# Weight unpacking with the shift inside the joining instruction, one score step for both heads, and a new order table

## The chip, the cores and the metric

The kernel runs on one core of a Trainium2 chip. The metric is the time of the program on the device, in microseconds (us). The engines are TensorE (PE, matmuls; its weight loads are PEld), VectorE (DVE), ScalarE (ACT), GpSimd (POOL) and SyncE (SP), which issues the DMAs here.

## The reference

Attention with two kinds of masks, then two dense layers with squared ReLU, then two with SiLU, all in float32 (B, H, S, D = 4, 8, 576, 64; the layers are 512 to 2048 to 512 over 2304 tokens):

```
scores = q @ k.T / sqrt(64)
rel = pos[:, None] - pos[None, :]
mask = (rel >= 0) & (rel < 32)                       # heads 0 to 3
mask = (rel >= 0) & (rel < 128) & (rel % 4 == 0)     # heads 4 to 7
attn = softmax(where(mask, scores, -1e9)) @ v        # heads side by side: x, 2304 x 512
h = x @ w_in;  x = (relu(h) * relu(h)) @ w_out       # first layer pair
h = x @ w_in2; out = (h * sigmoid(h)) @ w_out2       # second layer pair
```

The weights arrive as 64-bit words (float64), two 32-bit words each.

## The kernel before, in words

Every float32 matmul operand of the layers is split into a high and a low half that PE takes at full rate, and a product is three matmuls (high by high, high by low, low by high; lines 788 to 790, 836 to 838). The layers run over token tiles. The first three tiles of 256 tokens of the first layer pair (`mlp`) run together with the attention of the early tokens and with the loading of the weights; this is the first stage, to about 215 us. Then come three tiles of 512 with one level of Strassen's scheme (`mlp2`, to 480 us), and three tiles of 768 for the second layer pair (`strassen`, to the end).

The attention goes by half sequences (h from 0 to 7, 288 queries each) and pairs of heads. For a pair, the score matmuls (line 533) have 64 rows of contraction, one head in partitions 0 to 63 and the other in 64 to 127; a plain pair has three units, a dilated pair four. As float32 each of these matmuls is two in the trace. DVE masks the scores and takes their extremes (line 558, tiles `ap`, `ast`), for the first eight pairs a subtraction follows (lines 691 on DVE, 694 on POOL), then PE transposes, ACT takes the exponential, PE multiplies by the values (738, 625) and the result is normalised.

Weights are unpacked by `weights`, 64 pieces of 128 x 512: the DMA brings `raw`; the high word is scaled into `cv` (line 282 on ACT, 284 elsewhere, called top); the low word is scaled in place (290 on ACT, 292 elsewhere, called low); `cv` is shifted by 3 (302, or POOL's form on `raw`, 304); the sign is put in (311 or 314); and the low word is added (318, on DVE or POOL, called the join). A cast to the high half (245, 247, 249) and a subtraction for the low half (252) follow.

Nothing is scheduled on the chip by chance: `ORDER` is a table that lists all operations with the engine they run on (P for PE, A for ACT, V for DVE, G for POOL, D for a DMA issued by SP) and the place of their buffers; `F14` is 14 filler matmuls on PE (line 1245). Each engine runs its own entries in the order of the table, and waits for the data. A POOL entry also waits for the last DVE entry ahead of it that is marked as locking their port. `APART` names the half sequences whose score step is two operations, one for each head.

Of the kernel before, what the change touches and what calls it, by code (L numbers as in the profile page):

```python
# [12 lines left out]
I32 = mybir.dt.int32  # L13
# [164 lines left out]
class Kern:  # L178
# [76 lines left out]
    def weights(self, m, c, key, dkey, js=(0, 1)):  # L255
# [3 lines left out]
        for j in js:  # L259
# [10 lines left out]
            vi = lambda cv=cv: cv.tile.bitcast(I32)  # L270
# [37 lines left out]
            def sign(e, vi=vi, pair=pair, b=b):  # L308
# [9 lines left out]
            w = self.op({"DVE": c_dve(n), "Pool": c_pool2(n)}, lambda e, vi=vi, pair=pair: self.eng[e].tensor_tensor(  # L318
                out=vi(), in0=vi(), in1=pair(I32)[:, :, 0], op=ALU.add), [s, z], k, [], [cv, raw], "w" + at, True)
# [1040 lines left out]
P10@3 P36@28@1 V17 V50 P67@36@2 G20 A12 V38 A11 V49 V37 D65@156 V48 P13@0 V39 V68 V40 D95@152 P21@1 F3@3 V51 A22  # L1360
P41@2 A23 D96@160 V35 V14 P24@3 V71 A43 V15 G127@0 V70 A42 A16@2 V81 D398@196 V79 P52@1 V69 V82 P44@2 V80 A53
V25 A54 V72 A136@4 P55@0 V26 V45 V66 V46 A27 V83 D143@52 P98@40@3 V56 V138 A47@6 V57 P28@1 G129 P73@3 V100
A29@44 F3@2 V58 A74 V101 D160@76 P59@2 V111 A31@48 V99 P84@3 V32 A62 V30 A60 P75@0 A85 V102 V61 A128 F3@1 V63
V110 D152@56 P86@2 V76 V103 A137 V77 V112 P104@1 A78@8 V113 V87 F7@3 V97 V114 V88 A105 V130 D177@88 A89 P115@1
V139 P106@0 A116 V131 F1@2 P90@3 D169@80 P117@2 V140 A91@60 A93@64 A132@68 F5@1 V94 V92 A141@164 V107 V118
P400@3@1@72@0 V108 V119 D211@124 G133 A153@14 V109@12 V120 A162 V403 F2@2 V401 A145 P121@0 G142 V402 V410
D506@201 P404@2 V411 A122 A144@10 V123 V412 A154 V146 P1238@3 D186@92 V399 A161@2 V147 A170@0 V148 P413@1 A124
A405 V178@4 D220@128 A149@84 V125 V163 A1239@16 P406@0 V150 A414 A1240 V164 P415@2 A179 D194@108 V407 V155
P1244@3 A1241@6 V408 V165 A409@8 V416 V156 A166@100 D424@196 P507@0@1@96@1 V417 V1242 A418 V157 P1243 A1245@18
V167 A158@168 D151 V172 A1246 V510 A187@10 D134 P419@3 V159 P1250@2 A422@104 A420 V512 A1247@12 G189 V508 V423  # L1370
A513 V421 A171 D203@116 V1248 P426@3@0@112@2 V180 A1251@16 V173 A511 P1249 A509 V427 G174 V523 A1252 V428 A188
V429 V436 V438 A1253@14 P430@2 V525 A524 V437 V514 V521 A526 V515 V425 V1254 A522 P439@1 V190 A431 A516 V527
A517 V175@172 P432@3 V528 V176 A440 A529 P518@0 V530 A222 P441@2 V433 V181 A204@2 P531@1 P1255 V434 V442 A520
V182 A435@8 V443 V519 A533 V444 D539@196 A532 A183@120 V191 P534@3 A195@6 V184 P445@0 A537@12 A535 V446 P1256@1
A192@176 G197 V448 V536 A196 V447 D450@201 V449 V198 A205 V193 A1257@18 P540@0@3@20@3 A1258 V199 A1259@4 D237@40
A212@0 V1260 V554 A200@28 P1261 V556 G206 V545 A557 V558 V543 A555 D254@76 V541 V201 A559 P452@0@3@24@0 A542
V560 V207 A544 A546 V561 D538 V451 P1262@1 V208 D271@112 A562 A563 V547 V465 V548 V455 A549 V466 G550 V454
# [12 lines left out]
P640@3 A627 A1282 V628 V641 P1273 A608 V645 A1283@14 V615 V652 V629 G1284 V616 V654 A630 V643 V656 P1303 V289@2  # L1390
V617 A1305@18 A297@4 V291 V292 P618@0 A1295@6 P1285 A642 V1306 A646 V293 A619 A298 V283 P631@0 P1310@2 A657
V277@132 A653 V284 A632 D339@124 V1296 A285@40 P633@0 V278 A655 V299 P1297 A644 A634 D185 V647 V286 A294@136
A1307@14 V635 D666@201 P1316@1 A1311@16 V306@6 A1312 V648 V658 A636@10 V659 V1308 A660 V295 P1322@2 D287
V1550@12 A649 D637 V308 A1317@18 V1551@2 P661@0 A1313@0 P650@3 P1309 A662 V307 A315 V1314 V1552@112 A651 V324
A1318 P667@3@76@1 V1554@108 A1323@16 V1553 A1324 V300 A1319@8 P663@1 A314@10 V669 P668@0 V1555 V673 A664@2 V1320
P1328@2 V682 V671 V680 D694@196 A672 V684 V316 A674 P1334@3@0@1 V301 A670 A1329@18 V309 A302@72 D665 V675 A1330
P1315 V676 D253 A685 V677 A1559 V303 D330@92 A1331@12 A1556 P678@2 V1332 P1321 V323@0 A1325@14 V317 A681 A679
V1326 A683 P1340@2 V1562@8 A1335@16 A1336 V310 V686 P695@3@20@2 V1563@2 A1341@18 A1342 V687 V1560 A688 P696@2
V701 V703 G1564@116 V697 A702 P1333 V712 A311@144 V714 V1557 A1337@4 D1561 A704 V699 V710 P1327 A715 V325 A700
V1338 V716 V318 D1558 P689@3 A1343@14 V312 P1346@2 A698 A711 V705 V341 A690 V706 V1565 A717 P1352@3 V707  # L1400
A1347@16 A1348 V1566@36 A713 V1344 A319@68 V1567 P708@2 P1339 V326 A709 A1353@18 V320 A1568 D347@112 V718
# [12 lines left out]
P786@2 A1419@18 V371 A1420 P1393 V1603 A1397@8 A787@0 V1398 A1604 V1593 A374@6 D820@196 P1412@3 V1596 A1607
# [259 lines left out]
```

## Time and profile before

| | us |
|---|---|
| three runs | 848.31, 849.13, 851.52 (median 849.13) |
| the profiled execution | 849.5 |
| its span in the trace | 847.7 |
| PE, DVE, ACT, POOL busy in the span | 839.2, 638.8, 501.5, 122.2 |

Busy time of an engine is the union of its instructions; PE's matmuls overlap each other, so the step from one start to the next tells what one costs. A wait is put down to the engine that released it last.

### The profile page before, as it was taken

The numbers are of one execution on the slowest core, as the hardware profiler recorded it, in microseconds if no ns is written. First come the engines' busy times: TensorE is split into PE (matmuls) and PEld (weight loads), VectorE is DVE, ScalarE is ACT, GpSimd is POOL, SyncE is SP. The second block draws the span as 40 slices with busy tenths as digits, with TensorE's granted clock in tenths as the row PEclk, the third lists the DMA queues.
The fourth block names the chain that finished last, engine by engine and source line by source line (L and its number), as shares of the span: only waits on it lengthen the run. The fifth ranks groups of instructions, "written<-read, shape, count | busy, mean of one in ns | idle before, by whom it ended". The sixth has DMA issues, their size and how long they took to land.

```text
span 847.7 us, 16967 instructions
## 1 busy us (share of the span) xinstructions
PE 839.2 (99%) x6009; PEld 795.6 (94%) x6009; DVE 638.8 (75%) x1706; ACT 501.5 (59%) x1324; POOL 122.2 (14%) x142
## 2 busy tenths in 40 slices
PE   9989999999999999999999999999999999999998
PEld 7879999999989889889998999999999999999998
DVE  6999999888888698768899997578722488422765
ACT  5999988887666265334542566565445555345652
POOL 2220000101210202131201002102201111202020
PEclk9999999999999999999999999999999999999999
DMA  9585568879898888988999989889774774773441
GB/s 344 178 284 207 152 204 304 278 265 333 310 303 318 308 292 282 326 311 288 336 344 299 343 308 351 301 287 324 248 259 149 246 266 164 269 262 111 174 159 65
DMA packets 83603, 223.56 MB, mean 264 GB/s; under 512 B 8768, under 2 KB 18240, under 8 KB 83520
## 3 DMA queue, kind: packets, MB, share of 16 engines
q1 hardware_dynamic: 83520, 222.49, 75.2%
q8 instruction: 47, 0.77, 0.3%
q14 instruction: 36, 0.29, 0.1%
HBM read 172.13 MB, written 50.33 MB: 262 GB/s over the span
## 4 chain that ended last, share of the span: by engine, by line
PE 94%; ACT 3%; DVE 1%; issue 0%; POOL 0%; POOLq 0%; ACTq 0%
PE y L1094 17%; PE sa L1179 15%; PE s L936 15%; PE y L1179 6%; PE y L990 5%; PE y L991 5%; PE y L992 5%; PE sa L1094 4%; PE s L788 3%; PE s L789 2%; PE s L790 2%; PE ax L533 2%; PE y L836 2%; PE ax L625 2%; PE y L837 2%; PE y L838 2%
## 5 line engine op out<-in xcount | busy, mean ns | idle before, releaser
L245 ACT CAST hl<-gq 128x384 fp32r<-128x384 f32 x168 | 79.5, 513 | 58.7 <-PE sa L1179 28.6
L1094 PE MATMUL y<-xs,ws 128*128 128x384 f32 x552 | 107.5, 334 | 0.0
L252 DVE TENSOR_TENSOR hl<-gq,hl 128x384 fp32r<-128x384 f32 x144 | 78.9, 581 | 27.3 <-ACT hl L245 24.0
L1094 PEld LDWEIGHTS y<-xs,ws 128*128 128x128 f32 x552 | 96.6, 188 | 0.1
L1065 DVE TENSOR_TENSOR gq<-y,gq 128x384 f32<-128x384 f32 x46 | 25.0, 554 | 94.1 <-PE y L1094 82.9
L1070 ACT COPY gq<-y 128x384 f32<-128x384 f32 x92 | 42.7, 479 | 75.0 <-PE y L1094 67.6
L1179 PE MATMUL sa<-hl,wp 128*128 128x384 f32 x432 | 79.1, 334 | 0.0
L936 PE MATMUL s<-x,ws 128*128 128x256 f32 x576 | 76.2, 284 | 0.0
L990 PE MATMUL y<-g,w 128*128 128x512 f32 x192 | 76.2, 397 | 0.0
L1179 PEld LDWEIGHTS sa<-hl,wp 128*128 128x128 f32 x432 | 75.2, 188 | 0.0
L991 PE MATMUL y<-g,w 128*128 128x512 f32 x192 | 75.2, 392 | 0.0
L992 PE MATMUL y<-g,w 128*128 128x512 f32 x192 | 74.9, 390 | 0.0
L952 DVE TENSOR_TENSOR h<-s,h 128x512 f32<-128x512 f32 x96 | 59.4, 619 | 19.8 <-PE s L936 16.6
L936 PEld LDWEIGHTS s<-x,ws 128*128 128x128 f32 x576 | 72.2, 191 | 1.2
L245 ACT CAST g<-r 128x256 fp32r<-128x256 f32 (+1 forms) x86 | 42.9, 504 | 51.2 <-DVE r L972 42.8
L566 ACT ACTIVATE ap<-ap,ast 96x128 f32<-96x128 f32 (+3 forms) x168 | 62.2, 371 | 8.3 <-DVE ast L575 4.2
L788 PE MATMUL s<-x,w 128*128 128x256 f32 x192 | 56.4, 294 | 0.1
L790 PE MATMUL s<-x,w 128*128 128x256 f32 x192 | 54.3, 283 | 0.0
L789 PE MATMUL s<-x,w 128*128 128x256 f32 x192 | 54.2, 282 | 0.0
L1179 PE MATMUL y<-hl,sw 128*128 128x384 f32 x288 | 51.4, 334 | 0.0
L1179 PE MATMUL sa<-hl,sw 128*128 128x384 f32 x288 | 50.9, 334 | 0.0
L1179 PEld LDWEIGHTS y<-hl,sw 128*128 128x128 f32 x288 | 50.0, 188 | 0.0
(176 smaller groups left out, 2071.2 us busy)
## 6 DMA issues: line engine op xcount, KB each, us to landing
raw<-w SPq DMA_DIRECT2D x64, 512.0 KB, 6.3
ws<-w1x SPq DMA_DIRECT2D x48, 512.0 KB, 6.7
ws<-w2x SPq DMA_DIRECT2D x48, 512.0 KB, 5.4
sw<-w2y SPq DMA_DIRECT2D x48, 512.0 KB, 4.5
wa<-w1s SPq DMA_DIRECT2D x24, 512.0 KB, 6.8
wa<-w2s SPq DMA_DIRECT2D x24, 512.0 KB, 5.7
w1x<-st SPq DMA_DIRECT2D x16, 512.0 KB, 4.8
w2x<-st SPq DMA_DIRECT2D x16, 512.0 KB, 5.1
```

The costliest lines, as they stand in the source:

```text
L245: self.nc.scalar.copy(out=out, in_=in_)
L252: self.eng[eng].tensor_tensor(out=out, in0=a, in1=b, op=ALU.subtract)
L566: es.append(self.op({"ACT": c_act(nk) + 0.185}, lambda e, i=i, n=n, c=c, p=p, st=st: nc.scalar.activation(out=p.tile[:n, c], in_=p.tile[:n ...
L788: nc.tensor.matmul(o, wh.tile[:, s], xh, start=(kk == 0), stop=False)
L789: nc.tensor.matmul(o, wh.tile[:, s], xl, start=False, stop=False)
L790: nc.tensor.matmul(o, wl.tile[:, s], xh, start=False, stop=(kk == KC - 1))
L936: nc.tensor.matmul(bank.tile[:, o:o + 256], wp, xp, start=i == 0, stop=last, skip_group_check=True)
L990: nc.tensor.matmul(o, wh.tile[:, s], gh.tile, start=c == 0, stop=False)
L991: nc.tensor.matmul(o, wh.tile[:, s], gl.tile, start=False, stop=False)
L992: nc.tensor.matmul(o, wl.tile[:, s], gh.tile, start=False, stop=(c == NF - 1))
L1094: nc.tensor.matmul(o, w[part == 2].tile[:, kk * P:kk * P + P], x[b][part == 1].tile[:, kk * half:kk * half + half], start=new and not kk a ...
L1179: nc.tensor.matmul(o, u.tile[:, c * P:c * P + P], v.tile, start=new and not q and not part, stop=q == nf - 1 and part == 2, skip_group_che ...
```

## The change

The operation `low` is gone, 64 of them. The join is a single DVE instruction that shifts the low word right by 29 and combines it with `cv` by a bitwise or; it can no longer run on POOL. `APART` is empty, so the fourth half sequence (h = 3) issues its scores for both heads in one operation, the heads in turn. The order table is another one; it has 3899 entries where 3969 stood, 48 fillers instead of 53, other engines for some operations and other places of buffers.

```diff
-            def low(e, pair=pair):
-                x = pair(U32)[:, :, 0]
-                if e == "ACT":
-                    nc.scalar.activation(out=x.bitcast(I32), in_=x, func=AF.Copy, scale=2.0 ** -29)
-                else:
-                    self.eng[e].tensor_scalar(out=x.bitcast(I32), in0=x, scalar1=2.0 ** -29, scalar2=1.0,
-                                            op0=ALU.mult, op1=ALU.mult)
-
             a = self.op({"ACT": c_act(n) + 0.05, "Pool": c_pool1(n), "DVE": c_dve2(n)}, top, [load], k, [cv], [raw], "v" + at, True)
-            z = self.op({"ACT": c_act(n) + 0.05, "Pool": c_pool1(n), "DVE": c_dve2(n)}, low, [load], k, [], [raw], "z" + at, True)
...
-            w = self.op({"DVE": c_dve(n), "Pool": c_pool2(n)}, lambda e, vi=vi, pair=pair: self.eng[e].tensor_tensor(
-                out=vi(), in0=vi(), in1=pair(I32)[:, :, 0], op=ALU.add), [s, z], k, [], [cv, raw], "w" + at, True)
+            w = self.op({"DVE": c_dve(n)}, lambda e, vi=vi, pair=pair: nc.vector.scalar_tensor_tensor(
+                out=vi(U32), in0=pair(U32)[:, :, 0], scalar=29, in1=vi(U32), op0=ALU.logical_shift_right, op1=ALU.bitwise_or),
+                [s], k, [], [cv, raw], "w" + at, True)
...
-APART = (3,)
+APART = ()
...
-V1 A3958 G0 F14@0 D3@140 D2@132 D33@136 V4 D64@144 D126@24 P5@20@0 F15@2 V8 V7 D34@148 V6 V18 D135@32 V9 V19
+G0 V1 F6@0 D2@145 P5@76@0 V6 D33@71 P36@138@1 V7 V8 V9 P10@3 A11 A12 V17 F9@0 D64@167 V50 D126@81 A127@173 V38 V18 V19 V49 G20 P21@1 A22 A23 P67@94@2 V39 V37 V40 P41@0 A43 A42 V48 V51 P52@3 D34@54 D96@30 G128 D3@127 V4 P13@2 V82 V97 V129 V69 V35 V79 D134@153 A53 A54 D95@186 A135@199 V14 V68 V15 A16@180 V80 V70 P24@1 V25 V71 V26 P44@3 V45 A27 V136 V46 V72 P98@117@3
```

How the table moves instructions shows at three places (the changed program's lines are 8 to 12 lower). On PE, the scores of the second plain pair of h = 3 (`blk` is the block of queries, keys and values, `ap` the probabilities, `s` a bank of the first layer), before:

```order
L533 MATMUL ax<-blk 96x128 x3
L625 MATMUL ax<-ap,blk 64x96 x6
L533 MATMUL ax<-blk 96x128 x3
L788 MATMUL s<-x,w_1116 128x256
L789 MATMUL s<-x,w_1116 128x256
```

and after:

```order
L594 MATMUL ax<-ident,ap 128x96 x3
L525 MATMUL ax<-blk 96x128 x6
L617 MATMUL ax<-ap,blk 64x96 x6
L780 MATMUL s<-x,w_1109 128x256
```

The two rows of three have become one of six. On SP, the first DMAs of the program (`w_114`, `w_161` with 390 columns are blocks of values, those with 576 columns queries and keys, `raw` packed weights), before:

```order
L495 DMA w_114<-qkv 128x390
L495 DMA w_118<-qkv 128x576
L495 DMA w_120<-qkv 128x576
L495 DMA w_124<-qkv 128x576
L274 DMA raw<-w 128x512
```

and after:

```order
L487 DMA w_104<-qkv 128x576
L487 DMA w_121<-qkv 128x576
L487 DMA w_156<-qkv 128x576
L274 DMA raw<-w 128x512
L487 DMA w_212<-qkv 128x390
```

The first value block has gone behind three blocks of queries and keys. On PE the 14 and 15 fillers that stood ahead of and behind the first set of scores have become 6 and 9, the 9 behind the second set and one transpose. On DVE, the first weights (`cv` is the piece in work), before:

```order
L314 SCALAR_TENSOR_TENSOR cv<-cv,raw 128x512
L311 SCALAR_TENSOR_TENSOR cv<-raw,cv 128x512
L318 ISA cv<-raw,cv 128x1024 x2
L252 TENSOR_TENSOR x<-ax,x 128x4x8
L252 TENSOR_TENSOR x<-ax,x 128x4x64
```

and after:

```order
L309 SCALAR_TENSOR_TENSOR cv<-raw,cv 128x512
L302 SCALAR_TENSOR_TENSOR cv<-raw,cv 128x512
L293 TENSOR_SCALAR cv<-cv 128x512
L309 SCALAR_TENSOR_TENSOR cv<-raw,cv 128x512
L736 TENSOR_SCALAR ast<-ax 72x4
```

Lines 302 and 305 put the sign in after the change, line 293 shifts, and line 309 is the join, in the place of line 318.

## Rows read from the trace of the kernel before

**Rows 1.** Page, part 1: busy us (share of the span) xinstructions
```profile
PE 839.2 (99%) x6009; PEld 795.6 (94%) x6009; DVE 638.8 (75%) x1706; ACT 501.5 (59%) x1324; POOL 122.2 (14%) x142
```

**Rows 2.** Page, part 4: the chain that ended last, shares by engine
```profile
PE 94%; ACT 3%; DVE 1%; issue 0%; POOL 0%; POOLq 0%; ACTq 0%
```

**Rows 3.** Table by stretches; columns in its first line
```profile
core 0: us, PE busy (x) PEld busy (x) DVE busy (x) ACT busy (x) POOL busy (x), PEclk, DMA share, GB/s
0.00:10.00 10.00, 9.02 (x78) 6.88 (x79) 2.85 (x25) 1.95 (x4) 3.62 (x13) 1.00 0.80 268
10.00:70.00 60.00, 56.05 (x595) 50.18 (x594) 57.93 (x280) 56.77 (x184) 11.19 (x13) 1.00 0.77 276
70.00:150.00 80.00, 80.00 (x739) 76.52 (x737) 76.24 (x252) 71.77 (x236) 2.14 (x3) 1.00 0.62 207
...
480.00:848.00 368.00, 364.22 (x2084) 361.33 (x2082) 222.16 (x418) 193.61 (x384) 54.40 (x48) 1.00 0.67 233
```

**Rows 4.** Who PE waited for: us in total, times, longest
```profile
PE y L837 <- POOL g L252: 0.9, 1, 0.9
PE y L836 <- ACT g L245: 0.8, 1, 0.8
```

**Rows 5.** The chain in order of time: start us, us, what
```profile
80.03 1.12 PE ax L533 x12
94.96 0.82 PE ax L533 x6
...
104.92 1.40 PE ax L533 x15
121.29 0.86 PE ax L533 x8
...
195.58 0.83 PE ax L533 x12
...
222.69 0.87 PE ax L533 x16
```

**Rows 6.** PE's instructions in order of time: start us, us, engine, line
```profile
92.85 0.66 PE L602 MATMUL ax<-ident,ap 96*128 96x96 f32 x6
93.29 0.36 PE L836 MATMUL y<-g,w 128*128 128x256 f32 x1
93.49 0.28 PE L837 MATMUL y<-g,w 128*128 128x256 f32 x1
93.61 0.28 PE L838 MATMUL y<-g,w 128*128 128x256 f32 x1
```

**Rows 7.** Groups by line: xcount | busy us, mean ns | idle before
```profile
L318 DVE CUSTOM_DVE_ANT_0 cv<-raw,cv 128x1024 uint16<-128x1024 uint16 x62 | 42.5, 688 | 0.5
...
L311 DVE SCALAR_TENSOR_TENSOR cv<-raw,cv 128x512 int32<-128x512 int32 x52 | 35.5, 683 | 0.1
L290 ACT ACTIVATE raw<-raw 128x512 int32<-128x512 uint32 x50 | 33.2, 679 | 2.9 <-DMA raw<-w 2.9
...
L292 DVE TENSOR_SCALAR raw<-raw 128x512 int32<-128x512 uint32 x12 | 5.0, 421 | 0.0
...
L318 POOL TENSOR_TENSOR cv<-cv,raw 128x512 int32<-128x512 int32 x2 | 2.6, 1308 | 2.6 <-DVE ast L558 1.5 <-DVE gq L252 1.1
...
L252 DVE TENSOR_TENSOR hl<-gq,hl 128x384 fp32r<-128x384 f32 x144 | 78.9, 581 | 27.3 <-ACT hl L245 24.0 <-POOL hl L252 2.7
...
L252 POOL TENSOR_TENSOR hl<-gq,hl 128x384 fp32r<-128x384 f32 x24 | 25.7, 1076 | 155.2 <-DVE hl L252 53.5 <-ACT hl L245 45.2 <-DMA wa<-w2s 33.6
```

**Rows 8.** All engines' first instructions in order of time, [idle before <-releaser]
```profile
3.27 0.06 DVE L510 MEMSET w<- 128x6 f32 x1 [2.35 <-DMA w<-qkv]
...
4.09 1.49 PE L533 MATMUL y<-w 64*96 64x96 f32 x12
...
5.72 0.29 DVE L558 CUSTOM_DVE_ANT_0 ap<-y,mask 96x128 f32<-96x128 f32 x1 [2.39 <-PE y L533]
...
7.61 2.00 POOL L694 TENSOR_SCALAR ap<-ap,ast 96x96 f32<-96x96 f32 x3 [5.15 <-DVE ast L558]
...
9.11 0.29 DVE L558 CUSTOM_DVE_ANT_0 ap<-y,mask 96x128 f32<-96x128 f32 x1 [1.60 <-PE y L533]
```

More of the change, by code (lines that the diff above doesn't have):

```diff
@@ L1363 @@
[L1363 to L1377, printed above, removed]
@@ new lines @@
+A1241@141 V219 V443 G1242 D148 V220 A221@88 G222 V227 D540@124 P541@3@0@14@0 V546 V561 V548 A549 A562 V555 A556
+V228 V542 V544 A545 A547 A543 D178 F6@2 D254@112 D133 D291@80 D446@9 P448@1@2@160@3 V450 V449 V559 V451 P1243
+V557 V462 A558 A262@132 V452 D193 V461 P453@3 A454 A560 A229@188 P1250@0 A1251@201 A1252 V550 V551 V233 V552
+P553@1 A554 V459 V447 V460 P463@3 V563 V564 V234 V565 P566@0 V235 V230 P455@2 V456 V241 A464 P465@3 V466
+A1253@152 V1254 A567 P568@0 A236@96 P1255 V457 D246@156 V467 V458@197 A468 P469@1 V247@109 V237 V263 P1262@2
@@ new lines @@
+A860 V854 A864 V865 V866 V1434 V867 V855 V1446 V856 V2023@86 V2026@58 P1460@3 A1461@56 A1462 P1441 P1453 P1466@2
+A1641@93 V1642 V1492@40 V1458 A1463@8 A2024@124 A1467@13 A1468 P1472@3 A1473@42 A1469@48 A1474 A2021@100
+A1502@17 V1631 V1464 P1435 P1447 P868@3 V2022 V2029@44 V2025 A1475@22 V1476 P857@2 A858 D873@196 P1459 V869
+A2030@72 P874@2@3@60@0 V888 P1465 V1470 P1471 V879 V877 A880 V890 A891 V2015 V875 V1504@81 V2031 D2054@24
+D1644@116 A2016@112 A876 V886 A878 V1498@9 A887 P870@2 A871@34 A889 P1478@3 A1479@32 V881 V882 V1645@66 V883
@@ new lines @@
+A1675@15 A2195@40 A1069 P1083@3 A1084@196 V2183@129 P2193@0 P2194@3 P2208@1 V2196 V2187@47 V1676 V2197 V2198
+V1704@21 V2199 V2200@44 A2201@36 P1087@0@2@92@0 V1101 V1092 A2184@27 V2185 V1099 V1088 A1093 A1089 V1705 V1707
+V2172 V1103 A1708 A1100 D2084@50 P2169 V1090 A1102 A2212@104 P2209@3 V2202 V2213 D1684 D1677 D1085 D2085@65
+D1722@108 P2210@0 P2211@3 D1113@196 D2034@120 D2032@71 V2204@58 A1104 A1091 V1701@32 V1702 D2033 D2035 P2173
+P2186 A2188@88 A2205@112 D1703 D1714@97 A1715@13 V2214 V2206 V1709 V2215 V1105 V2189 V1094 V2216 V2217@41
@@ new lines @@
+P2309 A1165 P1166@3 V2332 V2319@92 V1150 V1151 A1167 V1152 P1153@1 V1732@54 A1734 V1154 V1741@29 D2269@76
+D1171@196 P1172@0@2@108@3 V1173 V1733 V1190 A1191 P1168@3 A1169@94 V1186 V1188 A1189 G1737 V1738 V1175 V1177
+V1742 D2270@36 D2272@70 D2267@3 V1192 A2320@31 V2321 A1727@46 V1728 P2329@1 P2330@3 P2344@2 P2322 V1179 V2333
+V2334 V1743 V2335 V2340@68 V1735 V2336@74 D2233 D2271@52 D2235 D1139 D2274@11 G2324@32 D1748@20 G1749@92 D2276@1
+D2277@58 A2348@201 P2345@0 V2349 P2346@2 P2347@0 P2361@1 V2350 V1744 V2325 V2351 A1193 V1750 V2352 P2362@3
@@ new lines @@
+V1200@52 V1759 D1201 V2385 P2360 P2381@2 P2373 V2386 V2387@73 V1768 V1769 V2391@34 D2285@112 D2238@28 A1763
+V1764 V1770 A2240@48 D2239 P2395@1 P2396@0 P2397@2 P2398@3 V2241 G2255@54 D2286@68 P2377 D2289@36 A2399@201
+A2392@196 V2400 A2242@76 A1760 V2401 D1765 V2246@24 A2388@12 A2247@44 P2412@1 A2416@20 V2249@2 V2252@114
+A2253@104 V2402 V2389 V1761 V1771@120 V2403 V2408@108 P2413@2 D2287@0 P2414@0 P2415@1 P2390 V2393 P2394 V2254
+V2417 V2418 A2409@60 A2256@36 V2404@9 V2410 V1772 G2248 V2419 V2420 V2421@26 A2422@68 D2465@100 D1774@4 V2243
@@ new lines @@
+P2517@2 P2531@1 A2438@10 V2503@68 A2504@72 V2510@13 V2519 V1821 V2505 V2520 V2521 P2506 P2507 D1788 D1791
+D1849@56 A1850@124 V1822 D2471@199 D2476@80 V1780 V2522 V2523@90 D1781 D2477@120 A2535@40 V1832@64 A2511@128
+V2512 A1823@203 V1851 A2524@116 V2525 V1852 V1853 P2532@3 P2533@0 P2534@2 V2536 P2508 P2509 P2513 V1834@96 V1833
+V2527@201 G1835 A1839 V2537 P2526 V1858@128 D1792@92 D2479@196 D1873@60 D2475@20 D1866@72 A2528@108 A1793@8
+V1856@164 V1857 V1794 V1859 V1824 V2538 V2539 V2529 A1863 A1836 D2478@28 P2548@3 P2549@0 P2550@2 V1864 A1860
@@ new lines @@
+V1861 A2552@199 V2553 P2551@1 P2565@0 A2569@20 D2481@4 D2435 P2530 D2483@68 D2491@2 D2433 D2480@169 P2566@3
+P2567@0 V2540@90 V1840 V2544@33 V1867@116 V1868 V1795 V2554 A2545@40 V1869 A2541@100 V2542 P2543 V1837 V2555
+V2546 V2556 D1865 D2482@85 A1874@70 P2568@1 V2561@178 V1875 A2562@180 V1796 V1876 V2570 D2439 D1897@81 A1898@94
+G1899 D2486@108 D2485@120 V1870 V1877 V2571 P2582@3 V2563 V2572 V2573 V2578@0 V1882@128 V2557@126 V1900
+A2558@197 V2559 V2574@102 P2547 D2440@172 D2484@90 P2583@0 P2584@1 P2585@2 D1862 D1841 V1880@72 D1838 D2437
@@ new lines @@
+A1983 A2746 V1974@108 V2843 P2844@1@2 V2846 P2783 A2784 P2847 V2764 A2785 D1814 A2782 P2786 V2787 P2788 P2790
+A2789@49 A1994@8 P2792 V2793 D2689@160 A2778 P2795@0 P2797 G2867 D1986@84 V1950@156 A2851@99 V2852 V1995 V2863
+V1951 V2880 V1996 V1984 A1987@91 V1997 V1988 A2868@113 A2791@52 P2799 P2802 A2800 V2780 A2798 D2690@34 P2804
+D2687@38 D2692@93 V2803 A2762 P2806 A2807@72 A2805@63 A2794 A2801 D1982 D2693@12 A2864@150 V1975 V2796 V1989
+P2808 V2809 A2769 A2848@143 V2849 V1990 V2865 V2000@66 V2001 P2811@3 P2813 A2814 P2815 P2818 A2816 A2817
@@ new lines @@
+A3037@2 A3053@72 P3008 P3011 P3014 P3017 P3020 P3023 V3040 V3030 A3033@128 V2650 A3041@161 V3034 V3048 V2998
+V3038 A3045@121 P3031 P3035 V3042 D3086@41 P3134 D3087@13 A3049@150 D3088@101 D2997 D3101@96 D3091@186 V3056
+V3026 V3054 P3039 D2999 A2658@55 A2653@87 P3043 A2651@112 V2652 V2660 V3050 A3057@124 V2655 V3024 V2654 V3046
+A2661@22 A3135@52 P3136 P3138@0 V2662 A2656@16 V2657 V3139 P3047 A3137@61 V2659 V2663 V3058 P3140 P3051
+D3089@127 D3090@0 D3092@136 P3142 P3144 P3055 A3141 V3143 P3146 A3145@68 A2664@28 V2665 A3147@71 P3148 P3151@0
@@ new lines @@
+A3253 A3280@175 D3118@22 P3267 P3270 D3119@14 D3123@104 V3278 V3289 V3272 D3061 D3120@55 D3121@88 D3128@100
+D3122@9 V3308 A3258 P3259 A3260 V3281 V3326 V3300 V3306 A3301@127 V3302 P3273 P3276 P3279 P3282 A3261 A3291@123
+A3297@64 A3246 A3309@30 V3312 A3323@77 A3313@3 A3327@74 V3292 P3286 P3290 P3293 A3294@190 V3298 P3299 P3303
+P3307 V3316 A3317@131 V3314 V3310 V3338 P3311 P3315 V3342 A3339@116 A3368@96 V3330 A3331@187 A3343@64 V3369
+V3400 V3334 A3335@6 V3318 V3350 A3351@128 A3426@31 A3359@0 P3319 A3295 A3362@172 V3324 P3325 V3352 V3346
@@ L1607 @@
+V3876 V3868 V3852 V3860 D3817 V3844 D3845 D3779 V3842 D3843 P3853 P3857 P3861 V3864 P3865 P3869 P3873 P3877
+A3878@21 D3879 V3780 D3781 P3880 P3881 P3882 P3883 P3884 P3885 P3886 P3887 A3888 D3889
 """
```

426 lines of the change are left out of this document (193 added, 233 removed).

## The prediction

> **What bounds the kernel now.** I read the busy shares first. The matrix engine (PE) is busy 839.2 of 847.7 us, the vector engine (DVE) 638.8, the scalar engine (ACT) 501.5, GpSimd (POOL) 122.2 [rows 1], and 94% of the chain that ended last is PE's [rows 2]. So an edit is worth what it takes off PE's own row of matmuls, or off the waits that PE still has. The table by stretches says where such waits can be: from 70 us on PE is full, in the first 70 it is not [rows 3]. The list of what PE waited for has eight entries; after the first microsecond the longest are 0.9 and 0.8 us [rows 4], and none over 0.3 lies behind 70 us. But PE's row there holds 53 filler matmuls and many short pieces, and the same table shows why: in 10 to 70 us DVE is busy 57.93 of 60 us and ACT 56.77 [rows 3]. I call this stretch the ramp: PE goes as fast as the two engines feed it. In 480 to 848 us DVE is busy 222 of 368 and ACT 194: nothing there waits for either.
>
> The profiled execution took 849.5 us, 1.8 beside its span of 847.7; the median of the runs is 849.13. I sum against 849.5 and take 0.37 off at the end. About 0.5% (4.25 us) is what a measurement of this kernel can tell from no change.
>
> **Scores of the fourth half sequence.** Before, head 0's score matmuls of a pair stand in a row, head 1's elsewhere; every other half sequence has them in turn. The chain shows both forms for the same shapes. One head of a plain pair takes 0.82 us (x6), twice; both heads in turn take 0.83 (x12). Another plain pair, whose two rows stand back to back, takes 1.12. A dilated pair takes 1.40 back to back, and 0.86 twice when parted; in turn it is 0.87 (x16) [rows 5]. The four pairs thus cost 1.12 + 1.64 + 1.40 + 1.72 = 5.88 before, and 2 x 0.83 + 2 x 0.87 = 3.40 after: -2.5 us. Two pairs were also parted by other work, so PE loses two changes of form: behind one, the next matmul's step is 0.20 instead of 0.12 us, and the entry costs as much [rows 6]; 2 x 0.15 makes **-2.8**. All of it lies at 80 to 125 us, where PE is full, so it is on the path.
>
> **Other changes of PE's row.** The order has 321 changes between kinds of matmuls instead of 348 and 48 fillers instead of 53; most of those changes cost no step. Adding both rows at the steps that the trace shows for each pair of neighbours gives 829.3 before and 826.1 after, 3.3 less, so **-0.5** beyond the scores.
>
> **The low words.** 64 instructions go. 50 stood on ACT (33.2 us), 12 on DVE (5.0) [rows 7], two on POOL. None is on PE, so directly they give 0. The join stays on DVE, in another form. The nearest rows are the old join (688 ns) and the joining of the sign, which has the new form, a shift or mask of a strided word and a second operand (683) [rows 7]: from -5 ns to nothing each; I take nothing. The two joins that stood on POOL (1308 ns there) now cost DVE 1.3 us together. What ACT gains is large: in its own queue the seventh product of the first stage now has 8 us less work ahead of it. But ACT was only one of the two engines that feed the ramp.
>
> **DVE in the ramp.** Here the order has to be read. Ahead of the low half that the seventh second-layer product needs, DVE has the same mix as before: 152 instructions of the masked reduction, 32 subtractions, 26 steps of the weights' sign and join where it had 25. At the trace's means that is 61.1 us of work against 61.5: no relief, since none of the twelve low-word conversions on DVE stood in those 61 us. Against PE's own row at full steps, DVE's work ran ahead by at most 1.8 us before (at the seventh product, 61.5 against 59.7), and by 2.6 after (at the tenth, 77.1 against 74.5): **+0.8** on PE's waiting.
>
> DVE's own idle time counts as much. By 70 us it is 9.2 us, of which 7.15 in the first ten [rows 3]. It starts on scores at 5.72, after PE's first set at 4.09, and waits 1.60 us again, until 9.11, for the second set [rows 8]. After, the first block to be loaded is the one that the first scores need (before, a value block was ahead of it, landing at 3.27), and the second set follows the first on PE at once. Its 295 KB instead of 200 first let it land near 3.5, and a set takes PE 1.4 to 1.5 us [rows 8]. So DVE can begin near 4.9 and need not stop until its twelve reductions are done, near 9.0. There it must wait: the third set of scores now stands behind a transpose that waits for three subtractions on POOL, 2.00 us [rows 8], beginning near 7.4. That gives scores near 10.5 and 1.5 us of idleness. 4.9 + 1.5 = 6.4, against 7.15 plus 0.4 up to the same point. I take 0.3 to 0.5 of the gain as kept, and as much again from ACT never being late in the ramp: **-0.8** together. Bounds: -3.5 (every idle stretch of DVE but its first 5 us and some latency goes) and +3.8 (below).
>
> **POOL's work.** The order leaves POOL 49 instructions of 142 in the trace, and some 35 us of DVE time take their place; in the last stage, for one, 18 subtractions of 1076 ns on POOL become 581 ns on DVE [rows 7], 10.5 us. DVE has 146 us free there [rows 3], and its results lie 30 us and more ahead of PE's need: 0. If that cover were gone, the same 10.5 us would be the price.
>
> **Sum.** -2.8 - 0.5 + 0.8 - 0.8 = -3.3: 846.2 for the profiled execution, **845.8** on the scale of the median, 0.4% faster.
>
> **Rivals.**
> First, the ramp shortens as well. If DVE starts 0.8 us earlier, loses the 1.60 us wait and finds no new one, the ramp ends 2.4 us earlier and the sum is -5.7: 843.4. For it: ACT's queue is 8 us shorter, and DVE idled 2.1 us between 10 and 70. Against it: POOL's three subtractions, and the 2.6 us margin.
>
> Second, slower: the new join is dearer than its nearest row. 18 joins stand ahead of the tenth product's low half, on an engine that is 97% busy, with the sign's step before and the cast behind each. Every 0.1 us more costs 1.8 us of ramp; 0.2 would make +3.6, about my upper bound. It decides from 4.25 + 3.3 = 7.6 us, 0.42 us a join (1.1 instead of 0.68). Twice the duration gives 18 x 0.68 = 12.2, less 3.3: 858.0. Against it stands the row of the sign's joining, the same form with the same strided operand at 683 ns, no more than the two-operand add at 688 [rows 7].
> The Trainium skill (Vector Engine (DVE) Microarchitecture Reference, "Points that are easy to get wrong") says that this form, with two operands in SBUF that aren't bf16, runs at half throughput. The trace doesn't agree: 683 ns against 688. By that rule the time would be the 858.0 above.
>
> Third, the change saves what it says and the ramp takes it back: PE's pieces get shorter while the margin of DVE grows, so that fillers and waits fill the room. With the table's +0.8 and DVE's idleness 2.5 us longer than I think, the sum is 0: 849.1.
>
> **Chances.** Forecast 0.53, first rival 0.33, slower join 0.08, taken back 0.06. The forecast's own spread reaches a little past 844.9, so: faster by over 0.5% 0.36, within 0.54, slower 0.10. The range takes in the first rival and its bound, 849.1 - 3.3 - 3.5 = 842.3, and on the other side -3.3 + 3.8, 849.6; it leaves out the dear join.
>
> **What would show it.** Right: every score set of that half sequence as one piece of 0.83 or 0.87 us; the join near 683 ns; ACT near 470 us busy, POOL near 38, DVE near 675; DVE still above 95% in 10 to 70 us; PE full from 75 us on. The first rival shows as a DVE that is less idle in the first 15 us and a PE that is through its first seven products near 67 instead of 70 us. Wrong: a join above 0.9 us, or PE waits of over 0.5 us behind 150 us, for a DMA or for DVE; then the moved work and the new places of the buffers cost what I set at nothing.

## The result, and the profile after

The changed kernel takes 853.79 us (median of six runs, 852.82 to 854.85) against 848.54 for the kernel before (six runs beside them): a ratio of 1.0056, 95% interval 1.0041 to 1.0071. It is 0.6% slower, where 0.4% faster was forecast, and outside the range (842.3 to 849.6). The profiled execution took 854.85 us with a span of 852.9, 5.2 more than the span before.

Parts 1 and 2 of the page after, the busy times and two rows of the 40 equal slices (21.3 us each):

```profile
PE 840.3 (99%) x6004; PEld 796.8 (93%) x6004; DVE 660.2 (77%) x1777; ACT 475.4 (56%) x1273; POOL 44.4 (5%) x49
...
PEclk9979999999999999999999999999999999999999
```

Beside [rows 1], DVE has 21 us more (36 was forecast), ACT 26 less and POOL 78 less, the last two about what the order promised; PE is as full as it was. What is new is the 7 in the third slice of the clock. The list of what PE waited for has its cause (us in total, times, longest), and can be laid beside [rows 4]:

```profile
PE ax L594 <- POOL ap L584: 3.1, 1, 3.1
PE y L525 <- DMA w<-qkv: 1.1, 1, 1.1
PE fill L1237 <- DVE warm L1229: 1.0, 1, 1.0
PE y L1086 <- ACT gq L1062: 0.8, 1, 0.8
```

One wait of 3.1 us stands ahead of the transposes of a normalised piece of the probabilities (line 594; the normalisation is line 584): half sequence 2, second pair, head 0, two units of 96x128, whose two multiplications the order leaves to POOL, as it did before. The table by stretches around it (columns as in [rows 3]):

```profile
0.00:10.00 10.00, 7.65 (x62) 5.73 (x63) 4.37 (x31) 2.89 (x6) 4.05 (x14) 1.00 0.76 260
10.00:70.00 60.00, 55.47 (x545) 50.55 (x545) 52.25 (x252) 46.87 (x161) 13.37 (x11) 0.91 0.72 259
...
52.00:54.00 2.00, 0.00 (x0) 0.00 (x0) 1.79 (x4) 0.00 (x0) 1.95 (x1) 0.66 1.02 405
54.00:62.00 8.00, 8.00 (x53) 7.64 (x54) 2.48 (x10) 3.85 (x11) 1.28 (x1) 0.50 0.65 262
62.00:64.00 2.00, 2.00 (x17) 2.00 (x16) 0.92 (x4) 0.68 (x2) 0.00 (x0) 0.78 0.00 0
64.00:70.00 6.00, 6.00 (x71) 5.34 (x70) 5.96 (x37) 5.49 (x22) 2.43 (x2) 1.00 0.02 4
```

Three things are to be seen in the last four rows. PE does nothing from 52 to 54 us. Then it is busy without a gap to 62, but at a granted clock of 0.50, the lower of its two levels (1.2 GHz), and gets 53 matmuls done in 8 us where it later does 71 in 6. And DVE, the engine that feeds this stretch, falls to 2.48 of 8 us, because PE no longer gives it anything to work on (its longest wait there is 4.9 us, for PE). Before, the clock was 1.00 in every stretch of this table.

Why did POOL take so long? Its instructions and DVE's there, in order of time (start us, us, engine, line, what), first DVE's:

```profile
49.31 0.26 DVE L550 CUSTOM_DVE_ANT_0 ap<-ax,mask 72x104 f32<-72x104 f32 x1
49.50 0.08 DVE L550 DVE_READ_ACCUMULATOR2_ANT ast<- 72x1 f32 x1
49.52 0.41 DVE L293 TENSOR_SCALAR cv<-cv 128x512 int32<-128x512 int32 x1
...
49.85 0.42 DVE L293 TENSOR_SCALAR cv<-cv 128x512 int32<-128x512 int32 x1
50.18 0.25 DVE L550 CUSTOM_DVE_ANT_0 ap<-ax,mask 72x104 f32<-72x104 f32 x1
...
50.37 1.28 DVE L302 SCALAR_TENSOR_TENSOR cv<-raw,cv 128x512 int32<-128x512 int32 x2
51.57 0.68 DVE L309 SCALAR_TENSOR_TENSOR cv<-raw,cv 128x512 uint32<-128x512 uint32 x1
52.17 0.68 DVE L252 TENSOR_TENSOR w<-cv,w 128x512 fp32r<-128x512 f32 x1
52.78 0.41 DVE L252 TENSOR_TENSOR g<-r,g 128x256 fp32r<-128x256 f32 x1
53.11 0.68 DVE L309 SCALAR_TENSOR_TENSOR cv<-raw,cv 128x512 uint32<-128x512 uint32 x1
```

and POOL's two multiplications (xcount: duration ns min/median/max, first and last start):

```profile
L584 POOL TENSOR_SCALAR ap<-ap,ast x2: 372/2418/4465, 49.1 to 49.5; 96x128 f32<-96x128 f32 x2
```

The first takes 372 ns. The second starts at 49.49, 30 ns before DVE begins its first instruction that has all its operands in SBUF, and ends 4.47 us later, 0.16 us behind the end of DVE's unbroken row (53.11 + 0.68 = 53.79). In the kernel before, the same two multiplications stood 1.5 us later, beside reductions (line 558, now 550) that DVE reads out of PSUM; its next instruction in SBUF alone began at 51.62:

```profile
50.62 0.72 POOL L592 TENSOR_SCALAR ap<-ap,ast 96x128 f32<-96x128 f32 x2 [3.07 <-ACT ap L590]
```

That reading gives a theory, A: POOL was shut out by DVE's row, through a port that both use; PE's standstill then cost the clock. Its rivals: B, the ramp is late anyway, for the joins and the work moved to DVE; C, POOL is slow there by itself.

### The profile page after: what moved, and what is told of

The parts are those of the page before. It is cut to its first block, busy times and chain, and to the rows that moved or that the text cites. A ratio compares the mean times of both kernels' runs of the same rounds, so it can differ in the third digit from the quotient of the medians.

```text
span 852.9 us, 16807 instructions
## 1 busy us (share of the span) xinstructions
PE 840.3 (99%) x6004; PEld 796.8 (93%) x6004; DVE 660.2 (77%) x1777; ACT 475.4 (56%) x1273; POOL 44.4 (5%) x49
## 4 chain that ended last, share of the span: by engine, by line
PE 93%; DVE 4%; DMA 1%; ACT 1%; POOL 1%; issue 0%; SPq 0%; DVEq 0%
PE y L1086 17%; PE sa L1171 15%; PE s L928 14%; PE y L1171 6%; PE y L982 5%; PE y L983 5%; PE y L984 5%; PE sa L1086 3%; PE s L780 2%; PE ax L525 2%; PE s L781 2%; PE s L782 2%; PE y L828 2%; PE ax L617 2%; PE y L829 2%; PE y L830 2%
## 5 line engine op out<-in xcount | busy, mean ns | idle before, releaser
L252 DVE TENSOR_TENSOR hl<-gq,hl 128x384 fp32r<-128x384 f32 x162 | 83.4, 552 | 26.3 <-ACT hl L245 25.9
L245 ACT CAST hl<-gq 128x384 fp32r<-128x384 f32 x168 | 77.7, 512 | 43.9 <-DVE gq L252 17.5
L245 ACT CAST g<-r 128x256 fp32r<-128x256 f32 (+1 forms) x94 | 46.5, 509 | 42.0 <-DVE r L964 25.8
L252 DVE TENSOR_TENSOR gq<-gq 128x384 f32<-128x384 f32 x94 | 51.8, 575 | 3.3 <-ACT gq L1122 3.0
L252 DVE TENSOR_TENSOR g<-r,g 128x256 fp32r<-128x256 f32 (+1 forms) x91 | 49.5, 549 | 3.5 <-ACT g L245 3.3
```

The lines of the kernel that those rows point to most:

```text
L245: self.nc.scalar.copy(out=out, in_=in_)
L252: self.eng[eng].tensor_tensor(out=out, in0=a, in1=b, op=ALU.subtract)
```

## The experiments

All are compared with the kernel before, in runs of their own beside it (849.0 to 849.4 us). Where two of them are set against each other, spans of the profiled executions are used too; the runs of one kernel are spread over 0.9 to 3.4 us.

**The normalisation on DVE.** One letter of the order table:

```diff
- ... V422 P1226@1 G518 V434 ...
+ ... V422 P1226@1 V518 V434 ...
```

> The changed kernel with one operation moved: the two normalising multiplications of 96x128 in front of the stalled transposes (the second of them took 4.47 us on POOL, and PE waited 3.1 us for it) are done by DVE. Theory A (POOL's second multiplication was shut out by DVE's unbroken row of instructions, and PE's standstill then cost the clock): no wait of over 0.5 us on PE between 45 and 60 us, the granted clock stays at 1.00 (2.4 GHz), and the 3.1 us of waiting and about 5.1 us (half of the 10.24 us at 0.50) both go: 852.9 - 8.2 gives a span near 844.7, a median of 845 to 846. Rival B (the ramp is late anyway, for the moved work and the joins on DVE; the POOL wait only stands in front of the next wait): another wait takes its place, the median stays at 851 to 854.

Measured: 847.58 us, ratio 0.9987 (0.9978 to 0.9996), span 845.6, 7.3 less than after. The wait is gone and the clock is 1.00. B falls: from 45 to 60 us nothing else was late by over 0.5 us. A and C are left. The gain is somewhat under the 8.2 that was expected, and the median above the 845 to 846. Two rows of this kernel's table by stretches are worth keeping, since they show the ramp without the stall:

```profile
0.00:10.00 10.00, 7.57 (x63) 5.81 (x64) 4.42 (x33) 2.77 (x6) 4.04 (x14) 1.00 0.81 268
10.00:70.00 60.00, 58.45 (x629) 53.49 (x629) 58.76 (x275) 52.04 (x177) 8.60 (x9) 1.00 0.76 264
```

By all the runs the same step is worth less than 7.3: the ratios 1.0056 and 0.9987 are 5.9 us apart. The five other runs of the changed kernel show a mean clock of 0.996 where the profiled one has 0.993, so the low clock cost less in them. The kernel before isn't free of it either: of the 33 runs beside this one, the one of 851.46 us had a mean clock of 0.996.

**DVE waits for POOL.** The order and the engines of the changed kernel stay; DVE's next instruction gets a wait on POOL's second multiplication:

```diff
+                if o is self.pl.ops[518]:
+                    held = [i for i in made[n:] if i.engine == mybir.EngineType.Pool][-1]
...
+                if held is not None:
+                    self.tc.add_manual_dep(next(i for i in made[n:] if i.engine == mybir.EngineType.DVE), held.name,
...
+                    held = None
```

> The changed kernel with one wait more and nothing moved: DVE's next instruction behind that normalisation waits until POOL has done both multiplications. Theory A (the port that POOL and DVE share): with DVE held, POOL needs about 0.4 us for each, as the first of them did (372 ns), DVE loses some 0.5 us, PE waits under 0.5 us, the clock stays at 1.00: 845.5 to 847. Rival C (POOL is slow there by itself, whatever DVE does): the second multiplication still takes over 4 us, PE still waits 3 us or more, and DVE's 4 us come on top: 854 to 858.

Measured: 848.35 us, ratio 0.9993 (0.9983 to 1.0002), span 846.0. POOL's pair, and DVE's instruction behind the wait:

```profile
49.11 0.72 POOL L584 TENSOR_SCALAR ap<-ap,ast 96x128 f32<-96x128 f32 x2 [7.66 <-DVE ast L550]
...
49.87 0.26 DVE L550 CUSTOM_DVE_ANT_0 ap<-ax,mask 72x104 f32<-72x104 f32 x1 [0.67 <-POOL ap L584]
```

It takes 0.72 for the two instead of 4.83. A wait of 0.67 us more on the busiest feeder made the kernel 6.9 us shorter by the span. C falls, though the median is 1.35 above the upper end of what A gave.

**Fillers in the wait.** `F28@3` ahead of the stalled transposes, POOL as it was.

> The changed kernel with 28 filler matmuls (256 columns, about 0.11 us each, 3.1 us together) on PE ahead of the stalled transposes; POOL's two multiplications stay as they are. It tells the wait from the clock. Theory A: PE reaches the stalled transpose as late as before, near 54 us, but it hasn't stood still, so that the granted clock stays at 1.00: only the clock's 5 us come back, 848 to 849.5. If the clock wasn't the cost, or falls all the same: 853 to 855.

Measured: 850.62 us, ratio 1.0018 (1.0009 to 1.0027), span 849.0. POOL's pair takes 4.83 again, but PE has something to do, by its instructions in order of time:

```profile
50.68 3.22 PE L1237 MATMUL fill<-warm 128*128 128x256 bf16 x28
```

and by the table by stretches:

```profile
50.00:54.00 4.00, 3.94 (x40) 3.35 (x38) 3.88 (x10) 1.23 (x5) 4.00 (x1) 1.00 1.03 406
54.00:62.00 8.00, 7.88 (x93) 7.16 (x93) 4.83 (x15) 5.90 (x17) 1.34 (x2) 1.00 0.68 276
```

From 54 to 62 us there are 93 matmuls instead of 53, at 1.00. So the 7.3 us part into 3.4 for the wait (849.0 against 845.6) and 3.9 for the clock (852.9 against 849.0); by the ratios it is 2.6 and 3.2. The median came out 1.1 above the upper end of what was expected: 5 us were to come back.

**Where POOL's instruction has to stand.** Two runs with the multiplications on POOL and no new wait. In the first, the last reduction goes ahead of the two shifts:

```diff
- ... V434 V421 P435@0 V419 ... V203 ... V211 V423 ...
+ ... V434 V421 V423 P435@0 V419 ... V203 ... V211 ...
```

> The changed kernel with one instruction of DVE's row moved and nothing else: the last of the masked reductions (PSUM and the mask, one operand in SBUF, 0.19 us to the next start) goes ahead of the two shifts of 128x512 in SBUF that DVE began 30 ns after POOL's first multiplication ended. POOL's pair stays on POOL and nobody waits for it anew. Theory A (POOL was shut out by the rows on SBUF that DVE began first): the second multiplication now begins beside that reduction, before the shifts, and takes 0.4 to 0.7 us; no wait of over 0.5 us on PE there, the clock stays at 1.00, span 845.5 to 846.5, median 847.5 to 848.5. Rival (any busy DVE, or POOL itself, makes it slow; the one held kernel was fast only since DVE stood still): it still takes 4 us and more, 852 to 854.

Measured: 854.17 us, ratio 1.0060 (1.0044 to 1.0077), span 852.6: no gain at all, against the expectation. POOL's pair, and the first shift on DVE:

```profile
49.23 4.83 POOL L584 TENSOR_SCALAR ap<-ap,ast 96x128 f32<-96x128 f32 x2 [7.62 <-DVE ast L550]
...
49.82 0.41 DVE L293 TENSOR_SCALAR cv<-cv 128x512 int32<-128x512 int32 x1
```

POOL's second multiplication began at 49.58, 0.24 us ahead of that shift, and was shut out nevertheless. Having begun first isn't enough. In the second run the reduction is done three times over, which writes the same result and moves the shift further away:

```diff
-            o.fn(o.eng)
+            for _ in range(3 if o is self.pl.ops[423] else 1):
+                o.fn(o.eng)
```

> The kernel of the run before (the last reduction ahead of the two shifts; POOL's second multiplication began 0.24 us before the first shift and was shut out all the same, 4.48 us) with that reduction done three times over, the same result written again: DVE stays busy, but its first instruction on SBUF alone begins some 0.6 us after POOL's second multiplication instead of 0.24. Theory A, sharpened (POOL's instruction needs about 0.37 us clear of DVE's instructions that read or write SBUF alone, from its start to its end, or it waits for the end of their whole row): it takes 0.37 us, PE waits under 0.5 us there, clock 1.00, span 846 to 847. Rival (any busy DVE shuts it out; it went well in the held kernel only since DVE stood still): 4 us and more again, 853 to 855.

Measured: 847.63 us, ratio 0.9983 (0.9974 to 0.9993), span 845.5. Again POOL's pair and the first shift:

```profile
48.90 0.72 POOL L584 TENSOR_SCALAR ap<-ap,ast 96x128 f32<-96x128 f32 x2 [7.68 <-DVE ast L550]
...
50.09 0.41 DVE L293 TENSOR_SCALAR cv<-cv 128x512 int32<-128x512 int32 x1
```

DVE now does two more reductions, and the kernel is 7.1 us shorter by the span than with one. It isn't DVE's being busy that shuts POOL out, but its row of instructions that work in SBUF alone; which forms in the row do it, these runs don't tell apart. With 0.84 us up to the first of them POOL's 0.37 us fit in, with 0.24 they did not. The kernel before has a small case of the same: of four multiplications of 72x72 on POOL at 275.6 us three take 0.32 us, and the one that began 0.02 us ahead of a shift and a two-operand instruction of DVE took 1.23 and ended 0.19 us behind the second. Nobody waited for it.

The Trainium skill (SBUF — State Buffer, "Who interferes with whom") says that GpSimd and VectorE share a pair of ports, taken by VectorE's instructions with two operands in SBUF (against a GpSimd instruction that reads SBUF) and by its two-port instructions, and that whichever is issued first has it for the whole instruction while the other blocks until that one ends. The first half of it agrees with these runs. By the start times of the trace the rest goes both ways: here POOL's instruction, begun 0.24 us earlier, lost, and then not to one instruction but to a whole row (in the changed kernel eight instructions in SBUF with a reduction among them, 4.3 us). But in the kernel before a subtraction of 128x384 on POOL at 721.12 us took its usual 1.01 us, and DVE's, begun 0.15 us later, took 1.27 instead of 0.55. Which of two near starts wins stays open.

**A stall made in the kernel before.** Ten small fills of an unused tile go between POOL's two multiplications of the same operation:

```diff
...
+                            if e == "Pool" and at == "2.1.0" and u:
+                                for _ in range(10):
+                                    nc.gpsimd.memset(self.sb.tile([96, 32], F32, tag="hold", name="hold", bufs=1), 0.0)
```

> The kernel before, with ten small fills (96x32, about 0.1 us each, of a tile that nothing reads) on POOL between the two multiplications of the same normalisation, which there stood beside DVE's reductions out of PSUM and took 0.72 us together. The second one now starts near 52.0 us instead of 51.0, in the middle of a row of DVE instructions on two SBUF operands, without a gap, that lasts until about 56.4 us. Theory A (the shared port, lost anew to each instruction of the row): it ends 2 to 5 us late, PE waits 1.5 to 5 us in front of its transposes, the granted clock falls if the wait is long enough: 851 to 858. Rival C (the stall is a property of the changed kernel, not of where POOL's instruction falls): the second multiplication takes 0.37 us again, PE waits about 0.9 us, and the time is 849 to 850.

Measured: 855.57 us, ratio 1.0072 (1.0056 to 1.0087), span 853.2 against 847.7. The time is the expected one, for another reason. POOL's instructions:

```profile
49.76 0.37 POOL L595 TENSOR_SCALAR ap<-ap,ast 96x128 f32<-96x128 f32 x1 [3.09 <-ACT ap L590]
50.08 2.40 POOL L594 MEMSET hold<- 96x32 f32 x10
52.45 0.51 POOL L595 TENSOR_SCALAR ap<-ap,ast 96x128 f32<-96x128 f32 x1
```

The ten fills took 2.40 us together, so the second multiplication began late, near the end of DVE's row, and was held up by one DVE instruction at most (0.51 us instead of 0.37). It doesn't show a multiplication shut out by a row. What it shows of the port lies in the fills: ns min/median/max, the longest of them, and DVE beside it:

```profile
L594 POOL MEMSET hold<- x10: 121/121/791, 50.1 to 52.4; 96x32 f32 x10
...
50.79 0.79 POOL L594 MEMSET hold<- 96x32 f32 x1
...
50.77 0.42 DVE L247 CAST w<-cv 128x512 fp32r<-128x512 f32 x1
51.10 0.41 DVE L302 TENSOR_SCALAR cv<-cv 128x512 int32<-128x512 int32 x1
51.44 0.68 DVE L252 TENSOR_TENSOR w<-cv,w 128x512 fp32r<-128x512 f32 x1
52.04 0.68 DVE L311 SCALAR_TENSOR_TENSOR cv<-raw,cv 128x512 int32<-128x512 int32 x1
```

Nine took 0.12 us. The one that began 0.02 us behind DVE's cast took 0.79, to 0.06 us behind the end of the shift that follows. The five after it took 0.12 again beside the two instructions with two operands, though these work in SBUF alone too. A fill reads nothing; POOL's multiplications, which do read SBUF, stayed shut out beside such instructions in the changed kernel.

On the clock the run says much; the longest of PE's waits:

```profile
PE ax L605 <- POOL ap L595: 2.1, 1, 2.1
```

and the ramp in the table by stretches:

```profile
10.00:70.00 60.00, 54.14 (x519) 48.90 (x519) 52.57 (x256) 52.01 (x168) 13.12 (x23) 0.91 0.73 255
```

2.1 us of standstill at this place cost the old order 5.5 us: the granted clock fell as it did after the change (0.91 on average in 10 to 70 us, in both), and the time with it. The loss belongs to the place, not to the change's instructions.

**The low words alone, in the old order.** The kernel before without the separate shift where the join is on DVE (62 of 64):

```diff
+                if w.eng == "DVE":
+                    return
...
+                if e == "DVE":
+                    nc.vector.scalar_tensor_tensor(out=vi().bitcast(U32), in0=pair(U32)[:, :, 0], scalar=29, in1=vi().bitcast(U32),
+                                                   op0=ALU.logical_shift_right, op1=ALU.bitwise_or)
```

> The kernel before with the low words' part of the change alone: where the join stands on DVE (62 of 64) the separate shift is left out and the join shifts; order table, scores and everything else as before. By the prediction's step the low words give nothing by themselves and at most 0.3 to 0.5 us through ACT in the first 70 us: 848.5 to 849.1. If ACT's relief is what shortens the first 70 us, up to 2.4 us come: 846.7. If the new join were dearer by more than its row says, DVE in the first 70 us would make it slower: over 850.

Measured: 848.68 us against 849.37, ratio 0.9991 (0.9982 to 1.0000); span 846.7 against 847.7. By the median and the span it is worth 0.7 to 1.0 us; the interval of the runs just reaches no change, but in the traces PE is 1.0 us ahead by 72 us and stays so to the end. The new join is not dearer; its group by line in the changed kernel, beside the 688 ns of [rows 7]:

```profile
L309 DVE SCALAR_TENSOR_TENSOR cv<-raw,cv 128x512 uint32<-128x512 uint32 x64 | 43.8, 688 | 0.6
```

**The low words undone in the new order.** The first of these kernels, with the shifts back, all 64 on ACT (50 before, see [rows 7]), and the old join:

```diff
+                z = pair(U32)[:, :, 0]
+                nc.scalar.activation(out=z.bitcast(I32), in_=z, func=AF.Copy, scale=2.0 ** -29)
...
```

> The first of these kernels (normalisation on DVE, new order) with the low words undone alone: all 64 are shifted by an instruction of ACT's again (some 0.68 us each, issued with the top word's step), and the join is the add of the kernel before. Everything else keeps its order. By the prediction's steps (the low words cost nothing themselves; ACT's relief is worth 0.3 to 0.5 us in the first 70 us) it should be at most 0.5 us slower than that kernel, 847.5 to 848.1. If ACT's relief is what made the first 70 us 2.4 us shorter, those come back and it is 2.4 us or more slower: 850 or above. The join stays near 0.68 us in both.

Measured: 859.43 us, ratio 1.0119 (1.0103 to 1.0136), 11.5 us more span than that kernel. The second expectation, 850 or above, holds, but the loss is nearly five times its 2.4 us. From 10 to 70 us:

```profile
10.00:70.00 60.00, 54.81 (x571) 49.03 (x567) 54.50 (x262) 56.87 (x183) 8.73 (x9) 1.00 0.73 257
```

ACT is as full as in the kernel before, but DVE does 54.50 us of work where it did 58.76: it waits for ACT (2.7 us), and so does PE (eight lines of its list of waits name ACT). The new order is built on an ACT that hasn't the low words to do; what nearly the same edit is worth depends on the order it stands in (1 us in the old one, 11.5 in the new).

**The scores in a row.** The first of these kernels, with the scores of h = 3 in one operation, but head 0's matmuls ahead of head 1's:

```diff
-            for i, (q0, n, k0, nk, m0) in enumerate(units):
-                for par in pars:
+            for par, i in [(par, i) for par in pars for i in range(nu)] if h == 3 else [(par, i) for i in range(nu) for par in pars]:
...
```

> The first of these kernels (normalisation on DVE) with the score matmuls of the fourth half sequence back to back, head 0's and then head 1's in the same operation, instead of in turn. By the trace of the kernel before (1.12 and 1.40 us back to back, 0.83 and 0.87 in turn, two pairs of each) it should be 2 x 0.29 + 2 x 0.53 = 1.6 us slower than that kernel, near 847; if order in turn is worth nothing on a full PE, no difference.

Measured: 848.58 us beside 847.58 in the same batch, spans 846.6 and 845.6: 1.0 us, where 1.6 was expected. By the ratios the two can't be told apart (0.9988 and 0.9987), so the weight lies on the traces. The chain of the changed kernel has two of the four pairs as single pieces (start us, us, what):

```profile
99.21 0.83 PE ax L525 x12
106.89 0.87 PE ax L525 x16
```

They are what [rows 5] promised. Added up over all steps of these matmuls, the pairs in a row cost 1.2 us more than in turn; PE's wait for a copy by DVE (0.42 us lost at 176.6 us in the kernel in turn) was gone in this one, and paid part of it.

**Four moves behind it.** What PE waits for at 500 us in the first of these kernels, by ACT's instructions in order of time:

```profile
498.86 1.28 ACT L1296 ACT_TABLE_LOAD   x1
...
500.73 0.48 ACT L1062 COPY gq<-y 128x384 f32<-128x384 f32 x1
```

The copy frees the bank that PE is to write, and stands behind a change of ACT's function table (entry A3891). It and three more entries (V243 is a join) are moved:

```diff
- A3891 V1952@108 V1803 A2636@22 A2725@16
+ V1952@108 V1803 A2636@22 A2725@16 A3891
...
- V1599@196 V842
+ V842 V1599@196
...
- A1649@28 P897@2 A898@98
+ P897@2 A898@98 A1649@28
...
- V243 A569 V570 A1263@92 A472 V473
+ A569 V570 A1263@92 A472 V473 V243
```

> The first of these kernels (normalisation on DVE) with four places of the order table changed where its trace shows PE waiting behind 70 us: ACT's change of function table (1.28 us, and a first activation) goes behind the copy that PE waits for at 500 us (1.01 us lost); two instructions of 0.69 and 0.60 us (DVE at 176.5, ACT at 212.1) go behind the copy that PE waits for (0.42 and 0.33 us lost); a join on DVE at 70.8 goes behind the two subtractions that PE's wait at 71.7 hangs on (0.56 lost). If each of these waits is the end of its own chain, 2.0 to 2.3 us come back: a span near 843.5, median near 845.5. If the next engine is as late each time, nothing: 847.6.

Measured: 845.82 us, ratio 0.9960 (0.9947 to 0.9973), span 843.5: all 2.1 us came back. PE's list of waits now starts with the first microseconds and has nothing over 0.6 us behind them:

```profile
PE y L525 <- DMA w<-qkv: 1.2, 1, 1.2
PE fill L1237 <- DVE warm L1229: 1.0, 1, 1.0
PE ax L525 <- PE ax L730: 0.6, 1, 0.6
```

This version beats both kernels: 0.4% under the one before, 0.95% under the changed one by the ratios.

## Why the prediction was wrong

By its own steps, against the spans (847.7 before, 852.9 after, 845.6 with the normalisation on DVE):

| step | forecast | measured |
|---|---|---|
| scores of h = 3 in turn | -2.8 | -2.4 (sum of the steps of all score matmuls, 845.6 kernel against before) |
| other changes of PE's row | -0.5 | not told apart (48 fillers instead of 53, 1.75 us less, are part of the ramp) |
| the ramp: margin +0.8, idle time -0.8 | 0 | -2.4 by DVE's work, -1.7 by PE's place at the end of the stage (below) |
| of it the low words | 0 direct | -1.0, alone in the old order |
| waits and places behind 70 us | 0 | +2.7 (or +2.0), not measured but what is left to the -2.1 of the 845.6 kernel; the four moves took back 2.1 |
| POOL's work | 0 | +7.3: 3.4 of wait, 3.9 of clock (+5.9 by all the runs) |

**The step that failed is "POOL's work: 0".** I weighed what POOL lost to DVE, in the last stage, and never what was left to it, though a POOL operation headed the list of PE's waits behind the first microsecond, with 0.9 us [rows 4]. The operation that PE stalled for was on POOL before and after, 0.72 us for the pair, and I carried that duration over. But that duration hung on DVE beside it: with POOL's pair 1.5 us earlier and DVE's row in SBUF 2.1 us earlier (49.52 against 51.62) it was 4.83. The kernel itself gave the hint, with an order in which a POOL entry waits for a marked DVE entry; but that is an entry ahead of it, and nothing keeps DVE's next row from coming in between the two multiplications. And of a 3 us wait I would have counted 3 us: the clock more than doubled it.

**The ramp went by the first rival.** It said that DVE starts earlier, loses its wait for the second set of scores, and gains 2.4 us. Its work in the first 70 us was 2.85 + 57.93 = 60.78 before [rows 3], and is 4.42 + 58.76 = 63.18 with the normalisation on DVE: 2.40 more done in the same time. PE bears it out in part: the 384th of its second-layer matmuls in the first stage begins at 162.5 us instead of 167.4, 4.9 us ahead, but the two orders differ there, and at the last matmul of the first layer in that stage (211.0 against 215.1) it is 4.1. Beside the scores' gain that leaves 1.7 to 2.5. DVE's first reduction came at 5.22, between the 4.9 forecast and the 5.72 before [rows 8]. The prediction had the mechanism and gave it 0.33; the margin of +0.8 that it set against it didn't show.

**What it set at nothing behind 70 us wasn't nothing.** It named the sign, waits of PE over 0.5 us behind 150 us, for a DMA or for DVE, and there are two: 0.77 us for DVE at 177 us, 0.42 of it lost, and 0.84 for ACT, which it hadn't named, 1.0 us lost at 500 us, where ACT changes its function table between two copies that PE needs (the table stood behind them before). The one for DVE and two smaller ones, 0.56 and 0.33 us lost, are of the same kind: an instruction that nobody waits for stands ahead of one that PE does.

**Right were** the size of the scores' pieces (0.83 and 0.87), the join (688 ns against 683 to 688), ACT's busy time (475 against 470), and roughly POOL's (44 against 38, 4 of it the stall) and DVE's (660 against 675). So the second rival, the dear join, is refuted, and with it the doubling that the prediction drew from the Trainium skill's rule of half throughput (Vector Engine (DVE) Microarchitecture Reference, "Points that are easy to get wrong"): 62 joins of that form alone, in the old order, made the kernel 1.0 us shorter, not longer. The times of the second and third rivals, 858.0 and 849.1, lie about equally far from the outcome, but neither mechanism was at work: DVE did more in the ramp, not less, once the stall was gone. Two slips in the prediction's sums change nothing: 829.3 less 826.1 is 3.2, not 3.3, and the bound of +3.8 refers to a sum that gives 3.6.

Without the failing step the span is 845.6, against 847.7 - 3.3 = 844.4 forecast; that this is so near is partly luck, as the ramp's gain and the loss behind 70 us, both set at 0, about cancel. What stays open: how often the low clock comes in full in the changed kernel (its runs show mean clocks of 0.993 and 0.996), which forms of DVE's row shut a POOL multiplication out, and who wins when both begin within some 0.2 us.

## What to carry to other kernels

What an operation on POOL takes can depend on DVE beside it, so when a change shifts DVE's row in time, look at each POOL operation that PE or DVE waits for, and at what DVE does beside it, from its start to its end: a duration taken beside the old neighbours needn't hold. A short wait on a full PE may cost the clock as well (those of 2.1 and 3.1 us did, the one of 0.84 us at 501 us did not): look at the granted clock behind it before counting its length alone. And when a new order loses where the parts should gain, move the one operation that is waited for before doubting the parts: here one letter of the table was worth 6 to 7 us, and four more moves 2.

## What the runs showed of the hardware that was not expected

A POOL multiplication of 96x128 takes 0.37 us beside DVE reductions out of PSUM, and 4.47 us when a gapless row of DVE instructions in SBUF begins 0.03 us after its start, or 0.24 us after (4.48). It gets no turn between the instructions of the row, and ends 0.15 to 0.16 us behind the last. DVE can lose too: its subtraction begun 0.15 us behind POOL's took 1.27 us instead of 0.55. A standstill of PE of 2.1 us, in a program that otherwise keeps it full, was followed by some 10 us at 0.50, and one of 3.1 us by the same. A POOL fill of 96x32 takes 0.12 us, also beside DVE instructions with two operands in SBUF, and took 0.79 when a cast on DVE, with a shift close behind it, began 0.02 us before it. ACT's change of function table takes 1.28 us, and its place in the row was worth a microsecond here.
